# Attention, gated experts and a cosine MLP on one core: the code for the smallest slot count stands right behind its test

## The chip, the core and the metric

The kernel runs on one core of a Trainium2 chip. The metric is the device time of one execution in microseconds; lower is better. The engines are TensorE (PE in the rows, its weight loads PEld), VectorE (DVE), ScalarE (ACT), GpSimd (POOL) and SyncE (SP), which issues most transfers. A name with a q behind it (PEldq, SPq) is the engine's sequencer, the part that reads the instructions in order and deals with waits, register loads, tests and jumps.

## The reference

```
attn = softmax(q k^T / 8 + bias(position))           # 2 batches, 8 heads, 576 positions, 64 wide
x    = (attn v), heads side by side                   # 1152 tokens x 512
logits = x w_gate + log(1 + exp(x w_noise)) * noise   # 8 experts
the two largest logits of a token choose its experts; softmax over the two gives their weights
x    = sum of both: weight * relu(x w1[e]) w2[e]      # 512 -> 1024 -> 512
h    = x w_in;  out = (h cos(h)) w_out                # 512 -> 2048 -> 512
```

How many tokens an expert gets depends on the data.

## The kernel before

The first part is the attention for all 1152 tokens, in tiles of 128 tokens. While it runs, each tile's gate is computed, the two experts of a token are chosen, and a slot in the list of each of them is counted out; GpSimd then scatters the token's row to those slots in a DRAM buffer (`xg`, line 840). Each expert has room for C = 320 slots.

The second part is `experts(bctx, W, ahead)`. It runs the eight experts over W slots each, expert by expert and in each over eight blocks of 128 hidden units: twelve matmuls (each operand is split into a high and a low part) into the tile H, a relu into `hhl`, twelve matmuls into the tiles Y. The weights of each block come by SyncE (`wraw`, line 1025) and are split by ScalarE (lines 1032 and 1040) and VectorE (1036, 1042). Beside this it already loads (line 1051) and converts weights of the last part. The slots of expert 1 and later are loaded from `xg` (line 1094); expert 0's input and its first three weight blocks lie on the chip when the attention part ends. The cosine MLP follows within the same function, with three token groups, and the last four stores to the output are issued by SyncE (line 1279).

The order of instructions on each engine is fixed while the program is built, by a small planner (`Plan`) that costs every step. It knows nothing of the tests.

The matmuls of the experts take as many columns as slots are computed. So the body is built three times, for 304, 312 and 320 slots (`WIDTHS` and C), and a fourth time for 320 slots with an extra part in front, which takes what an expert gets beyond 320. Which one runs is decided on the chip: `total_i` holds the largest count of any expert (written on VectorE at line 853), every engine loads it into a register (line 1351) and tests it (lines 1352, 1353 and 1411). In each engine's stream the blocks stand one behind the other as they are written: extra part and 320, then 320, then 312, then 304, then the end of the program, with semaphores and a barrier of all engines (under the line of the surrounding context, 1499). At the end of each body a jump leads to that common end. In this input the 304-slot body runs.

Of the kernel before, what the change touches and what calls it, by code (L numbers as in the profile page):

```python
# [8 lines left out]
F32 = mybir.dt.float32  # L9
# [4 lines left out]
AF = mybir.ActivationFunctionType  # L14
OP = mybir.AluOpType
AX = mybir.AxisListType
PSUM = bass.MemoryType.PSUM

B, H, S, D = 2, 8, 576, 64
DM = H * D  # L20
NT = B * S
HID = 32
E = 8
F = 1024
FB = F // 128
# [4 lines left out]
NTILE = NT // 128  # L30
C = 320
WIDTHS = (C - 16, C - 8)
# [133 lines left out]
def attention_moe_cosine_mlp_kernel(  # L166
# [5 lines left out]
    nc = tc.nc  # L172
# [11 lines left out]
    yd = dram.tile([ROWS, DM], F32, name="yd")  # L184
    xd = dram.tile([NT, DM], F32, name="xd")
# [16 lines left out]
    ident = const.tile([128, 128], F32, name="ident")  # L202
    carry = const.tile([128, NTILE + 1, E], F32, name="carry")
    oh = const.tile([128, NTILE, 2, E], BF16, name="oh")
# [6 lines left out]
    total = const.tile([128, E + 1], F32, name="total")  # L211
    total_i = const.tile([128, 2, E + 1], I32, name="total_i")
# [13 lines left out]
    with ExitStack() as actx:  # L226
        pool = actx.enter_context(tc.tile_pool(name="attn", bufs=1))
# [5 lines left out]
                     t=[128, S], m=[128, 1], e0=[128, 640], e1=[128, S], et=[128, 4, 128], etl=[128, 128],  # L233
                     ot=[128, 4, 128], rs=[128, H], x=[128, DM], lgs=[128, 128], rt=None,
                     bias=[128, H, S])
        bufs = dict(S=2, etp=2, aux=2, qraw=2, kraw=2, feat=5, bst=2, t=3, m=4, e0=2, e1=2, et=4, etl=2, ot=2, rs=3,
                    x=3, lgs=1, rt=2, qt=3, bias=2, raw=RAWS)
# [1111 lines left out]


    most = nc.values_load(total_i[0:1, 0, E:E + 1], min_val=0, max_val=2 * NT)
    with tc.If(most > WIDTHS[1]) as more:
        with tc.If(most > C) as over:
            with tc.tile_pool(name="ovf", bufs=1) as pool, tc.tile_pool(name="ps_o", bufs=2, space=PSUM) as ps_o:
                within = pool.tile([128, NTILE, E], F32, name="within")
                nc.vector.tensor_tensor(within, carry[:, 1:NTILE + 1, :],
                                        carry[:, 0:1, :].to_broadcast([128, NTILE, E]), op=OP.subtract)
                nc.vector.tensor_scalar(within, within, float(C), None, op0=OP.is_le)
                nc.vector.tensor_reduce(total[:, 0:E], within.rearrange("p t e -> p e t"), axis=AX.X, op=OP.add)
                nc.vector.tensor_copy(total_i[:, 1, 0:E], total[:, 0:E])  # L1360
                acc = pool.tile([128, NTILE, 2, DM], F32, name="oacc")
                nc.vector.memset(acc, 0.0)
                for e in range(E):
                    count = nc.values_load(total_i[0:1, 0, e:e + 1], min_val=0, max_val=NT)
                    with tc.If(count > C):
                        w = pool.tile([128, FB, 2, 512], F32, name="ow")
                        for f in range(FB):
                            nc.sync.dma_start(w[:, f], mwp[e * FB + f].rearrange("p (a d) -> p a d", a=2))
                        t0 = nc.values_load(total_i[0:1, 1, e:e + 1], min_val=0, max_val=NTILE - 1)
                        with tc.For_i(t0, NTILE) as t:  # L1370
                            x = pool.tile([128, 4, 128], F32, name="ox")
                            src = xd[bass.ds(t * 128, 128), :]
                            if e == 0:
                                nc.sync.dma_start(x, src.rearrange("p (c s) -> p c s", c=4))
                            else:
                                src = src.rearrange("p (i c b) -> p c i b", i=4, c=4)
                                for c in range(4):
                                    nc.sync.dma_start(x[:, c].rearrange("p (i b) -> p i b", i=4), src[:, c])
                            hotf = pool.tile([128, 2, E], F32, name="ohot")
                            nc.vector.tensor_copy(hotf, oh[:, bass.ds(t, 1), :, :].rearrange("p o j e -> p (o j) e"))  # L1380
                            ps = ps_o.tile([128, 512], F32, name="otr")
                            for c in range(4):
                                nc.tensor.transpose(ps[:, c * 128:(c + 1) * 128], x[:, c, :], ident)
                            xT = pool.tile([128, 4, 128], F32, name="oxT")
                            nc.vector.tensor_copy(xT.rearrange("p c s -> p (c s)"), ps)
                            py = ps_o.tile([128, 512], F32, name="opy")
                            for f in range(FB):
                                ph = ps_o.tile([128, 512], F32, name="oph")
                                for c in range(4):
                                    nc.tensor.matmul(ph[:, 0:128], w[:, f, 0, c * 128:(c + 1) * 128], xT[:, c, :],  # L1390
                                                     start=(c == 0), stop=(c == 3))
                                hT = pool.tile([128, 128], F32, name="ohT", bufs=2)
                                nc.scalar.activation(hT, ph[:, 0:128], AF.Relu)
                                nc.tensor.matmul(py, hT, w[:, f, 1, :], start=(f == 0), stop=(f == FB - 1))
                            a = acc[:, bass.ds(t, 1), :, :].rearrange("p o j (i c b) -> p (o j) c i b", i=4, c=4)
                            yv = py.rearrange("p (c i b) -> p c i b", c=4, i=4)
                            for j in range(2):
                                for c in range(4):
                                    nc.vector.scalar_tensor_tensor(a[:, j, c], yv[:, c], hotf[:, j, e:e + 1], a[:, j, c],
                                                                   op0=OP.mult, op1=OP.add)  # L1400
                for j in range(2):
                    r = j * NT
                    nc.sync.dma_start(yd[r:r + NT, :].rearrange("(t p) d -> p t d", p=128), acc[:, :, j, :])

            with ExitStack() as bctx:
                experts(bctx, C, False)
        with over.Else():
            with ExitStack() as bctx:
                experts(bctx, C)
    with more.Else():  # L1410
        with tc.If(most > WIDTHS[0]) as some:
            with ExitStack() as bctx:
                experts(bctx, WIDTHS[1])
        with some.Else():
            with ExitStack() as bctx:
                experts(bctx, WIDTHS[0])


# [84 lines left out]
```

## Time and profile before

| | us |
|---|---|
| median of 3 runs | 681.82 (681.18 to 684.2) |
| profiled execution, its own time | 689.02 |
| span of the profiled execution | 687.2 |
| TensorE busy | 632.1 (92%) |
| VectorE busy | 510.0 (74%) |
| ScalarE busy | 395.6 (58%) |
| GpSimd busy | 107.1 (16%) |

The span runs from the first to the last instruction of the profiled execution. Busy times do not count register loads, tests, jumps and semaphores; such instructions are on record by line, though, with their start and duration. An "issue" wait is time in which an engine waited for nothing that the profile shows as work. The granted clock of TensorE (PEclk) is a share of 2.4 GHz; the mean over the span is 0.982, and it has two levels, 1 and 0.5. "q8 instruction" and "q14 instruction" are the DMA queues that bring instructions to the engines; a packet of the first has 16 KB, one of the second 8 KB.

### The profile page before, as it was taken

To read this page: it belongs to the slowest core of one execution; us is meant where nothing else is said; L and a number is where in the kernel's file an instruction comes from. 1 tells how busy PE (TensorE), PEld (TensorE's weight loads), DVE (VectorE), ACT (ScalarE), POOL (GpSimd) and SP (SyncE) were. 2 spreads that over 40 slices of the span, in tenths; PEclk is the share of its full clock that TensorE was granted. 3 is DMA by queue.
4 is the path that set the end of the run, shared out by engine and by line. 5 is a ranking of instruction groups with operands and counts; after the bars stand their busy time and mean duration, and the time that the engine had idled before them with its cause. 6 is when DMAs were issued, how large, how long until landed. Compare 5 with 4: busy or idle time off the path is not lost.

```text
span 687.2 us, 12766 instructions
## 1 busy us (share of the span) xinstructions
PE 632.1 (92%) x4678; PEld 552.3 (80%) x4678; DVE 510.0 (74%) x1271; ACT 395.6 (58%) x791; POOL 107.1 (16%) x179
## 2 busy tenths in 40 slices
PE   5778998898899849999998998999999999999996
PEld 1346676675578649999998998999999999999996
DVE  6796897898878637989969888766998545554443
ACT  5666687777668525666645646544665444444333
POOL 4140124313222210002100011021400040001000
PEclk9998999999999959999999999999999999999999
DMA  5858788676658329698897897974730040001001
GB/s 174 207 162 255 247 281 270 214 217 199 204 165 267 106 73 279 189 302 269 238 301 211 250 281 207 250 201 157 240 100 25 0 138 1 1 7 40 1 1 46
DMA packets 58177, 116.45 MB, mean 169 GB/s; under 512 B 7024, under 2 KB 26864, under 8 KB 56048
## 3 DMA queue, kind: packets, MB, share of 16 engines
q1 hardware_dynamic: 54544, 104.41, 51.1%
q0 software_dynamic: 3552, 11.04, 4.8%
q8 instruction: 41, 0.67, 0.4%
q14 instruction: 40, 0.33, 0.2%
HBM read 78.12 MB, written 32.58 MB: 161 GB/s over the span
## 4 chain that ended last, share of the span: by engine, by line
PE 51%; DMA 6%; DVE 5%; issue 2%; ACT 1%; SPq 0%; DVEq 0%; POOL 0%; ACTq 0%
PE H L1002 25%; PE Y L1002 25%; DMA wraw<-in_mwp_dram 3%; DMA io<-xg 2%; DVE qt L1042 1%; DVE whl L1042 1%; DVE io L1153 1%; DMA xg<-x,token 1%; PE H L1191 1%; DMA bias<-xg 1%; DVE s L1072 1%; DVE s L1103 0%; ACT qt L1040 0%; DVE hhl L1133 0%; DVE qraw L1108 0%
## 5 line engine op out<-in xcount | busy, mean ns | idle before, releaser
L1002 PE MATMUL Y<-hhl,qt 128*128 128x304 f32 x468 | 73.3, 302 | 4.3 <-DVE hhl L1133 4.1
L1002 PE MATMUL Y<-w,hhl 128*128 128x512 f32 (+1 forms) x330 | 74.8, 372 | 0.0
L1002 PEld LDWEIGHTS Y<-hhl,qt 128*128 128x128 f32 x468 | 66.8, 188 | 5.6 <-DVE hhl L1133 5.5
L1002 PEld LDWEIGHTS Y<-w,hhl 128*128 128x128 f32 x330 | 56.7, 188 | 8.7
L503 ACT ACTIVATE e<-t,m 128x576 f32<-128x576 f32 x72 | 55.5, 771 | 11.8 <-DVE m L494 10.6
L489 PE MATMUL S<-kt,qt 128*128 128x288 f32 x320 | 59.0, 313 | 2.9 <-DVE m L494 2.9
L494 DVE CUSTOM_DVE_ANT_0 t<-S,bias 128x576 f32<-128x576 f32 x72 | 53.4, 750 | 9.4 <-DMA bias<-e 2.7
L1002 PE MATMUL H<-qraw,qt 128*128 128x304 f32 (+1 forms) x300 | 50.9, 321 | 8.3 <-issue 8.3
L1002 PEld LDWEIGHTS H<-qraw,qt 128*128 128x128 f32 x300 | 47.9, 199 | 9.1 <-issue 8.6
L489 PEld LDWEIGHTS S<-kt,qt 128*128 128x128 f32 x320 | 45.1, 190 | 8.5 <-DVE m L494 4.1
L1131 ACT ACTIVATE hhl<-H 128x304 fp32r<-128x304 f32 x64 | 26.7, 417 | 40.3 <-PE H L1002 38.4
L1002 PE MATMUL H<-qraw,w 128*128 128x384 f32 x264 | 49.3, 336 | 0.0
L1242 ACT ACTIVATE u<-H 128x384 f32<-128x384 f32 (+1 forms) x52 | 23.8, 466 | 42.2 <-PE H L1002 40.3
L1002 PEld LDWEIGHTS H<-qraw,w 128*128 128x128 f32 x264 | 46.6, 188 | 1.7
L510 PE MATMUL etp<-ident,e 128*128 128x128 f32 x288 | 44.6, 278 | 3.3 <-ACT e L503 2.6
L538 PE MATMUL aux<-et,vt 128*64 128x128 f32 (+1 forms) x640 | 42.5, 277 | 5.5 <-DMA vt<-in_vd_dram 3.2
L1042 DVE TENSOR_TENSOR qt<-wraw,qt 128x1024 fp32r<-128x1024 f32 x35 | 42.7, 1224 | 6.2 <-ACT qt L1040 5.6
L1002 PE MATMUL Y<-hhl,whl 128*128 128x304 f32 x300 | 45.6, 300 | 0.0
L1248 ACT ACTIVATE u<-u 128x384 f32<-128x384 f32 (+1 forms) x52 | 25.7, 498 | 34.1 <-DVE u L1246 33.8
L538 PEld LDWEIGHTS aux<-et,vt 128*64 128x64 f32 x640 | 33.2, 143 | 13.7 <-DMA vt<-in_vd_dram 3.5
L1254 DVE TENSOR_TENSOR hhl<-u,hhl 128x384 fp32r<-128x384 f32 (+1 forms) x52 | 27.2, 526 | 22.7 <-ACT hhl L1252 22.0
L1040 ACT ACTIVATE qt<-wraw 128x1024 fp32r<-128x1024 f32 x36 | 37.7, 1053 | 10.5 <-DMA wraw<-in_mwp_dram 6.1
(206 smaller groups left out, 1372.6 us busy)
## 6 DMA issues: line engine op xcount, KB each, us to landing
wraw<-in_mwp_dram SPq DMA_DIRECT2D x64, 512.0 KB
r<-in_mw2p_dram SPq DMA_DIRECT2D x16, 1024.0 KB
dist<-bst SPq DMA_DIRECT2D x24, 295.5 KB
bias<-dist SPq DMA_DIRECT2D x24, 288.0 KB
xg<-zero SPq DMA_DIRECT2D x20, 256.0 KB
yd<-zero SPq DMA_DIRECT2D x20, 256.0 KB
yd<-io SPq DMA_DIRECT2D x32, 160.0 KB
io<-xg SPq DMA_DIRECT2D x28, 160.0 KB
```

Source lines behind the costliest of these rows:

```text
L489: nc.tensor.matmul(s[:, hf, 0:HF], tl("qt", (it, bb))[:, u, h, :], kt[:, bb, h, hf * HF:hf * HF + HF], start=(i == 0), stop=(i == len(term ...
L494: nc.vector.tensor_tensor_reduce(out=tl("t", n).rearrange("p (a j) -> p a j", a=2), in0=tl("S", n)[:, :, 0:HF], in1=tl("bias", it)[:, h, : ...
L503: P.op({"ACT": 0.76}, lambda e: nc.scalar.activation(tl(*ek)[:, 0:S], tl("t", n), AF.Exp, bias=tl("m", n), scale=-1.0, accum_out=tl("rs", ...
L510: nc.tensor.transpose(tl("etp", n)[:, j * 128:(j + 1) * 128], tl(*ek)[:, j * 128:(j + 1) * 128], ident)
L538: nc.tensor.matmul(tl(*ax2)[h0, q0], lw, rx, start=(s == 0), stop=(s == 4))
L1002: nc.tensor.matmul(out_, lw(a), rx(b_), start=(first and i == 0), stop=(last and i == n - 1))
L1040: P.op({"ACT": 0.947}, lambda e: nc.scalar.activation(wt(i)[:, 0], tl(*rk), AF.Copy), pr, r=[rk], w=[wname(i) + (0,)])
L1042: P.op({"DVE": 1.135, "POOL": 2.4}, lambda e: (nc.gpsimd if e == "POOL" else nc.vector).tensor_tensor(wt(i)[:, 1], tl(*rk), wt(i)[:, 0].bi ...
L1131: P.op({"ACT": 0.053 + 0.00083 * W}, lambda en: nc.scalar.activation(tl(*hk)[:, 0, 0:W], tl(*pk)[:, 0:W], AF.Relu), g + 0.3, r=ks, w=[hk + ...
L1242: P.op({"ACT": 0.06 + 0.00083 * m}, lambda e: nc.scalar.activation(u(), h(), AF.Copy, scale=1.0 / (2.0 * math.pi), bias=0.25), z, r=ks, w= ...
L1248: P.op({"ACT": 0.187 + 0.00083 * m}, lambda e: nc.scalar.activation(u(), u(), AF.Sin, scale=2.0 * math.pi), z + 0.04, r=[un[1]], w=[un[2]])
L1254: P.op({"DVE": 0.069 + 0.00104 * m}, lambda e: nc.vector.tensor_tensor(part(1), u(), part(0).bitcast(F32), op=OP.subtract), z + 0.07, r=[u ...
```

## The change

The tests are turned around and nested the other way. The first asks whether the largest count is at most 304, and the 304-slot body stands right behind it; then 312, then 320, and what goes beyond 320 comes last. The code of the four bodies is the same, the extra part is only indented differently (its lines are left out here).

```diff
     most = nc.values_load(total_i[0:1, 0, E:E + 1], min_val=0, max_val=2 * NT)
-    with tc.If(most > WIDTHS[1]) as more:
-        with tc.If(most > C) as over:
-            with tc.tile_pool(name="ovf", bufs=1) as pool, tc.tile_pool(name="ps_o", bufs=2, space=PSUM) as ps_o:
...
-            with ExitStack() as bctx:
-                experts(bctx, C, False)
-        with over.Else():
-            with ExitStack() as bctx:
-                experts(bctx, C)
-    with more.Else():
-        with tc.If(most > WIDTHS[0]) as some:
+
+    with tc.If(most <= WIDTHS[0]) as few:
+        with ExitStack() as bctx:
+            experts(bctx, WIDTHS[0])
+    with few.Else():
+        with tc.If(most <= WIDTHS[1]) as some:
             with ExitStack() as bctx:
                 experts(bctx, WIDTHS[1])
         with some.Else():
-            with ExitStack() as bctx:
-                experts(bctx, WIDTHS[0])
+            with tc.If(most <= C) as full:
+                with ExitStack() as bctx:
+                    experts(bctx, C)
+            with full.Else():
+                with tc.tile_pool(name="ovf", bufs=1) as pool, tc.tile_pool(name="ps_o", bufs=2, space=PSUM) as ps_o:
...
+                with ExitStack() as bctx:
+                    experts(bctx, C, False)
```

In TensorE's stream, the place where the count is loaded and tested, with what stands before and behind the jumps (H and Y are the tiles in PSUM, `qraw` holds the input of expert 0, `qt` the weights of the first three blocks). Before; behind the first dots come the end of the 320-slot body, the second test and the start of the 312-slot body, behind the second dots the end of the 312-slot body and the start of the 304-slot body:

```order
L639 MATMUL etp<-t,x 128x64 x8
L657 MATMUL S<-ident 128x128 x4
L1351 TENSOR_LOAD total_i
L1352 COMPARE_AND_BRANCH
L1353 COMPARE_AND_BRANCH
L1364 TENSOR_LOAD total_i
...
L1353 UNCONDITIONAL_BRANCH
L1411 COMPARE_AND_BRANCH
L1002 MATMUL H<-qraw,qt 128x312 x30
...
L1411 UNCONDITIONAL_BRANCH
L1002 MATMUL H<-qraw,qt 128x304 x30
```

In the changed kernel the same place of TensorE's stream reads:

```order
L639 MATMUL etp<-t,x 128x64 x8
L657 MATMUL S<-ident 128x128 x4
L1351 TENSOR_LOAD total_i
L1353 COMPARE_AND_BRANCH
L1002 MATMUL H<-qraw,qt 128x304 x30
L1002 MATMUL Y<-hhl,qt 128x304 x12
L1002 MATMUL H<-qraw,qt 128x304 x6
L1002 MATMUL Y<-hhl,qt 128x304 x12
```

Before, the way from the first test (L1352) to the 304-slot matmuls leads over two jumps; now these matmuls stand behind the one test (L1353).

In SyncE's stream, the end of the 304-slot body. Before, these are the last rows, and the common end of the program follows:

```order
L1051 DMA r_20459<-in_mw2p_dram 128x2048
L1051 DMA r_20561<-in_mw2p_dram 128x2048
L1279 DMA out_dram<-s 16x8x512 x2
L1279 DMA out_dram<-s 16x8x256 x2
L1411 UNCONDITIONAL_BRANCH
```

In the changed kernel the 312-slot body follows, then the other two:

```order
L1051 DMA r_6523<-in_mw2p_dram 128x2048
L1279 DMA out_dram<-s 16x8x512 x2
L1279 DMA out_dram<-s 16x8x256 x2
L1353 UNCONDITIONAL_BRANCH
L1357 COMPARE_AND_BRANCH
L1051 DMA r_7988<-in_mw2p_dram 128x2048
L1025 DMA wraw<-in_mwp_dram 128x1024 x2
```

The jump at the end of the body (L1411 before, L1353 now) went to the next instructions of the stream and now goes past three bodies.

## Rows read from the trace of the kernel before

**Rows 1.** The page: the span.
```profile
span 687.2 us, 12766 instructions
```

**Rows 2.** Chain of waits, 236 to 262 us: start, duration, what.
```profile
244.00 1.88 PE S L657 x8
245.88 8.29 issue
254.18 7.18 PE H L1002 x30
```

**Rows 3.** Table of waits, 243 to 262 us: who, for what, total, times, longest.
```profile
ACT whl L1032 <- issue: 10.2, 1, 10.2
...
PE H L1002 <- issue: 8.3, 1, 8.3
```

**Rows 4.** Line 1351: ns min/median/max, first and last start in us.
```profile
L1351 PEldq TENSOR_LOAD <-total_i x1: 487/487/487, 244.8 to 244.8; - x1
```

**Rows 5.** Line 1352, the first test.
```profile
L1352 ACTq COMPARE_BRANCH  x1: 50/50/50, 245.4 to 245.4; - x1
L1352 PEldq COMPARE_BRANCH  x1: 3458/3458/3458, 245.4 to 245.4; - x1
L1352 SPq COMPARE_BRANCH  x1: 50/50/50, 245.7 to 245.7; - x1
```

**Rows 6.** Line 1411, the second test.
```profile
L1411 ACTq COMPARE_BRANCH  x1: 45/45/45, 248.3 to 248.3; - x1
L1411 PEldq COMPARE_BRANCH  x1: 4948/4948/4948, 249.0 to 249.0; - x1
L1411 SPq COMPARE_BRANCH  x1: 45/45/45, 249.3 to 249.3; - x1
```

**Rows 7.** First instructions behind it: lines 1032, 1499 and 1002, 244 to 260 us.
```profile
L1032 ACTq EVENT_SEMAPHORE  x3: 38/38/38, 254.4 to 254.6; - x3
...
L1499 SPq EVENT_SEMAPHORE  x3: 17/17/17, 255.0 to 259.8; - x3
...
L1002 PE MATMUL H<-qraw,qt x11: 455/455/592, 254.2 to 256.8; 128*128 128x304 f32 x11
```

**Rows 8.** DMA queues, 242:254, then 262:670, then 670:688: packets, MB, share.
```profile
q14 instruction: 11, 0.09, 5.4%
q8 instruction: 3, 0.05, 2.7%
...
q8 instruction: 20, 0.33, 0.3%
...
q1 hardware_dynamic: 576, 0.79, 14.7%
```

**Rows 9.** Stretches: length, busy PE, PEld, DVE, ACT, POOL; PEclk, DMA share, GB/s.
```profile
59.00:60.00 1.00, 0.11 (x2) 0.11 (x4) 0.00 (x0) 0.00 (x0) 0.00 (x0) 0.50 0.96 245
65.00:66.00 1.00, 1.00 (x9) 0.83 (x5) 0.79 (x1) 0.86 (x4) 0.00 (x0) 0.62 0.10 37
243.00:244.00 1.00, 1.00 (x8) 1.00 (x8) 0.63 (x2) 0.34 (x1) 0.00 (x0) 0.63 0.00 0
260.00:261.00 1.00, 1.00 (x8) 1.00 (x7) 0.00 (x0) 0.42 (x1) 0.00 (x0) 0.84 0.41 135
```

**Rows 10.** The end: lines 1352 and 1499, and SyncE's waits.
```profile
L1352 ACTq EVENT_SEMAPHORE  x1: 17/17/17, 682.0 to 682.0; - x1
L1352 SPq EVENT_SEMAPHORE  x1: 17/17/17, 683.9 to 683.9; - x1
...
L1499 SPq EVENT_SEMAPHORE  x2: 28/28/28, 686.2 to 686.3; - x2
...
SPq L1499 <- DMA out_dram<-s: 1.7, 1, 1.7
```

**Rows 11.** Stretches, columns as in rows 9: the scatter over, the 1 MB load.
```profile
251.00:252.00 1.00, 0.00 (x0) 0.00 (x0) 0.00 (x0) 0.00 (x0) 0.00 (x0) 0.50 0.00 0
256.00:260.00 4.00, 4.00 (x18) 4.00 (x17) 2.74 (x4) 2.64 (x5) 0.00 (x0) 0.50 0.79 268
```

More of the change, by code (lines that the diff above doesn't have):

```diff
@@ L1351, in attention_moe_cosine_mlp_kernel @@
     most = nc.values_load(total_i[0:1, 0, E:E + 1], min_val=0, max_val=2 * NT)
-    with tc.If(most > WIDTHS[1]) as more:
-        with tc.If(most > C) as over:
-            with tc.tile_pool(name="ovf", bufs=1) as pool, tc.tile_pool(name="ps_o", bufs=2, space=PSUM) as ps_o:
[L1355 to L1403, printed above, removed]
-            with ExitStack() as bctx:
-                experts(bctx, C, False)
-        with over.Else():
-            with ExitStack() as bctx:
-                experts(bctx, C)
@@ L1414, in attention_moe_cosine_mlp_kernel @@
         with some.Else():
-            with ExitStack() as bctx:
-                experts(bctx, WIDTHS[0])
+            with tc.If(most <= C) as full:
[3 more added lines that the diff above has]
+                with tc.tile_pool(name="ovf", bufs=1) as pool, tc.tile_pool(name="ps_o", bufs=2, space=PSUM) as ps_o:
+                    within = pool.tile([128, NTILE, E], F32, name="within")
+                    nc.vector.tensor_tensor(within, carry[:, 1:NTILE + 1, :],
+                                            carry[:, 0:1, :].to_broadcast([128, NTILE, E]), op=OP.subtract)
+                    nc.vector.tensor_scalar(within, within, float(C), None, op0=OP.is_le)
+                    nc.vector.tensor_reduce(total[:, 0:E], within.rearrange("p t e -> p e t"), axis=AX.X, op=OP.add)
+                    nc.vector.tensor_copy(total_i[:, 1, 0:E], total[:, 0:E])
+                    acc = pool.tile([128, NTILE, 2, DM], F32, name="oacc")
+                    nc.vector.memset(acc, 0.0)
+                    for e in range(E):
+                        count = nc.values_load(total_i[0:1, 0, e:e + 1], min_val=0, max_val=NT)
+                        with tc.If(count > C):
+                            w = pool.tile([128, FB, 2, 512], F32, name="ow")
+                            for f in range(FB):
+                                nc.sync.dma_start(w[:, f], mwp[e * FB + f].rearrange("p (a d) -> p a d", a=2))
+                            t0 = nc.values_load(total_i[0:1, 1, e:e + 1], min_val=0, max_val=NTILE - 1)
+                            with tc.For_i(t0, NTILE) as t:
+                                x = pool.tile([128, 4, 128], F32, name="ox")
+                                src = xd[bass.ds(t * 128, 128), :]
+                                if e == 0:
+                                    nc.sync.dma_start(x, src.rearrange("p (c s) -> p c s", c=4))
+                                else:
+                                    src = src.rearrange("p (i c b) -> p c i b", i=4, c=4)
+                                    for c in range(4):
+                                        nc.sync.dma_start(x[:, c].rearrange("p (i b) -> p i b", i=4), src[:, c])
+                                hotf = pool.tile([128, 2, E], F32, name="ohot")
+                                nc.vector.tensor_copy(hotf, oh[:, bass.ds(t, 1), :, :].rearrange("p o j e -> p (o j) e"))
+                                ps = ps_o.tile([128, 512], F32, name="otr")
+                                for c in range(4):
+                                    nc.tensor.transpose(ps[:, c * 128:(c + 1) * 128], x[:, c, :], ident)
+                                xT = pool.tile([128, 4, 128], F32, name="oxT")
+                                nc.vector.tensor_copy(xT.rearrange("p c s -> p (c s)"), ps)
+                                py = ps_o.tile([128, 512], F32, name="opy")
+                                for f in range(FB):
+                                    ph = ps_o.tile([128, 512], F32, name="oph")
+                                    for c in range(4):
+                                        nc.tensor.matmul(ph[:, 0:128], w[:, f, 0, c * 128:(c + 1) * 128], xT[:, c, :],
+                                                         start=(c == 0), stop=(c == 3))
+                                    hT = pool.tile([128, 128], F32, name="ohT", bufs=2)
+                                    nc.scalar.activation(hT, ph[:, 0:128], AF.Relu)
+                                    nc.tensor.matmul(py, hT, w[:, f, 1, :], start=(f == 0), stop=(f == FB - 1))
+                                a = acc[:, bass.ds(t, 1), :, :].rearrange("p o j (i c b) -> p (o j) c i b", i=4, c=4)
+                                yv = py.rearrange("p (c i b) -> p c i b", c=4, i=4)
+                                for j in range(2):
+                                    for c in range(4):
+                                        nc.vector.scalar_tensor_tensor(a[:, j, c], yv[:, c], hotf[:, j, e:e + 1], a[:, j, c],
+                                                                       op0=OP.mult, op1=OP.add)
+                    for j in range(2):
+                        r = j * NT
+                        nc.sync.dma_start(yd[r:r + NT, :].rearrange("(t p) d -> p t d", p=128), acc[:, :, j, :])
+                with ExitStack() as bctx:
+                    experts(bctx, C, False)
```

## The prediction

> **What bounds the kernel now.** I read the chain of waits first. Around the change it goes from TensorE's last matmul of the attention part (L657, over at 245.88 us) through 8.29 us of "issue" to the first expert matmul at 254.18 [rows 2]. From there to the end the chain is TensorE work with short gaps, so an expert part that starts earlier ends earlier. The table of waits says the same by engine: TensorE idle 8.3 us, ScalarE 10.2 us, both for "issue", that is, for nothing that another engine or a transfer owes them [rows 3]; VectorE in its turn waits for ScalarE there.
>
> The rows of the branch lines say what the "issue" is. The count is loaded at 244.8 in 0.49 us on TensorE's sequencer [rows 4]. The first test follows at 245.4 and is on record with 3458 ns on TensorE; the second starts at 249.0 with 4948 ns, so it is over at 253.95 [rows 5, 6]. On ScalarE and SyncE a test itself takes 45 to 50 ns, but the next instruction comes much later: on ScalarE the tests start at 245.4 and 248.3 and the next instruction at 254.4; on SyncE at 245.7, 249.3 and 255.0 [rows 5 to 7]. So a taken jump costs 2.85 (ScalarE), 3.46 (TensorE) or 3.55 us (SyncE) the first time, and 4.95 (TensorE), 5.65 (SyncE) or 6.05 us (ScalarE) the second. In that stretch the two instruction queues of the DMA carry 14 packets in 12 us, and in the last 18 us of the run, where only near code is reached, none; only data moves [rows 8]. My reading: the jump itself is cheap, and what costs is bringing in code that lies far away.
>
> **The change, part by part.** *Head.* On every engine two tests, both jumping far, become one test that falls into the 304-slot code, which now stands right behind it. Load and test stay: on TensorE 245.4 for the test. Its last attention matmul ends at 245.88, so if falling through costs no more than the 45 to 50 ns of the test on the other engines, the first expert matmul starts at about 245.9 instead of 254.18: 8.3 us earlier. It needs nothing later: input and weights of the first three blocks are written in the attention part. The feeders move by more: ScalarE's first instruction from 254.4 to about 245.45 (9.0), SyncE's from 255.0 to 245.8 (9.2); VectorE's first work waits for ScalarE and moves with it. GpSimd's two scatters stand ahead of its test and stay.
>
> No row shows a test that is not taken, so its price lies between 0.05 us (the record of a test) and 3.46 us (a whole first jump on TensorE). I take the low end: what follows is the next instruction in the stream, and where the stream runs straight on, from 262 to 670, one instruction queue alone brings 20 packets [rows 8] while the table of waits of that stretch has no "issue" wait of TensorE.
>
> The clock adds something. TensorE's granted clock falls from 1 to 0.5 (from 2.4 to 1.2 GHz) at 243.3 (the mean 0.63 of that microsecond) and is back at 260.3 (mean 0.84), 6.1 us after the expert matmuls began; at the other such place it works again from 59.9 on and has full clock at 65.8, 5.9 us later [rows 9]. If the clock returns about 6 us after work starts again, and that start is the first matmul of the experts, all of it merely shifts, and full speed comes at 252.0. But now TensorE works on nearly without a break from 242.0; counted from there the clock is back at 247.9, which saves half of 4.1 us, 2.05. So 0 to 2.05. I take 0.5: ScalarE and VectorE move by only 9.0, and later TensorE stalls are waits for VectorE, so what goes beyond 9.0 is largely lost there. Head: 8.3 + 0.5 = **8.8 us gained**.
>
> *Tail.* The 304-slot code was the last in each engine's stream, and its end lay next to the common end of the program. Now three other bodies lie between, so each of the five engines makes one far jump at the end. Price: the same rows, 2.85 to 6.05 us. Who waits? TensorE, VectorE and ScalarE are done before SyncE: ScalarE's last semaphore before the end stands at 682.0, SyncE's at 683.9 [rows 10], so with equal jumps SyncE's ends last. SyncE issues the last stores, and now waits 1.7 us for them to land; from 686.3, when it has gone through its semaphores, 0.9 us of barrier lead to 687.2 [rows 1, 10]. A jump that starts at 683.9 runs beside the landing of the stores and covers that wait, so it is not added whole. I take 4.0 us: SyncE's first jump was 3.55, and here the stores keep the DMA busy. Then 687.9; some 14 semaphores of the common end, at the pace of the last ones about 0.05 each, 0.6; the barrier 0.9: 689.4 instead of 687.2, **2.2 us lost**. With 2.85 it is 1.1 lost, with 6.05 4.3.
>
> *Everything else.* The instructions of the 304-slot body are the same in number and order, so matmuls, transfers and waits within it shift as a block. The 1 MB load that opens SyncE's part now starts beside the last scatter; 268 GB/s over 256 to 260 us makes it some 4 us of DMA, the scatter's packets end before 251 [rows 11]; the loads that need the scatter come for the second expert only, so I cost this at nothing. Without that cover it could hold SyncE's queue for at most those 4 us.
>
> **Sum.** The profiled execution took 689.02 us with a span of 687.2 [rows 1]: 689.02 - 8.8 + 2.2 = 682.4, that is 6.6 us less. It stands 7.2 us above the median of the runs, 681.82; a code fetch should cost about the same in either, so I carry the difference over: 681.82 - 6.6 = **675.2 us**.
>
> [...]
>
> **The rivals.**
> 1. *A test costs its fetch even when not taken.* The head then gains 8.3 less one first jump of 2.85 to 3.46, about 5.1, the tail still loses 2.2: 678.9 us (678.6 to 679.2). For it: TensorE's record shows the long time on the test itself, not behind it. Against: on the other engines the test is 45 to 50 ns and the pause comes behind.
> 2. *The clock comes back early and its gain is kept.* Head 10.35, tail 1.1 to 2.2: 672.6 to 673.7 us. For it: no break in TensorE's work at the seam any more. Against: the later waits for VectorE.
> 3. *Jumps are cheap, and the long records are an effect of taking the profile.* Then an unprofiled run saves one test of 50 ns [rows 5]: 681.8 us, and the change does not do what it seems to. [...] Against: the engines really do nothing in 246 to 254, and the instruction queues move packets there.
> 4. *The start is held by the scatter, and the tail pays: slower.* SyncE's 1 MB load, started at 246, collides with the last scatter and pushes its landing from about 250 by up to 4 us to 254. If the first expert work waits on it, the head gains nothing (254.2), and an end jump at the upper price costs 4.3: 686.1 us. It decides once the first expert matmul comes later than about 252, that is, once the gain ahead falls under the 2.2 of the tail. For it: the scatter does end just ahead of the present start. Against: the wait table names no transfer ahead of the first matmul.
>
> That the count is above 304 in this input, so that other code is run, is out: the first expert matmuls have 304 columns [rows 7].
>
> **How the numbers follow.** Forecast 0.74, rival 1 0.09, rival 2 0.08, rival 3 0.05, rival 4 0.04. A measurement of this kernel can tell about 0.5% from no change, 3.4 us. Forecast and rival 2 are faster: 0.82. Rivals 1 and 3 end within it: 0.14. Slower: 0.04. The low end of the range is rival 2 at its best, 8.3 + 2.05 gained and 1.1 lost, 672.5. The worst of the forecast's own bounds is 8.3 - 4.3 = 4.0 gained, 677.8; reaching to the near edge of rival 1 gives 678.6. Left out are most of rival 1, rivals 3 and 4, and a little of the scatter of runs: under 2 in 10.
>
> **What would show it.** In the changed profile: one test per engine, of some 50 ns; TensorE's first expert matmul at about 246, ScalarE's first conversion at 245.7; few instruction packets in 242 to 254; full clock by 252 at the latest. At the end SyncE's last stores some 8.8 us earlier, at about 675, then a pause of 3 to 6 us on SyncE with instruction packets in it, and no wait for the stores. Wrong would be: a pause of several us behind the test (rival 1), a first matmul that waits for a transfer (rival 4), an end where TensorE's or ScalarE's jump ends after SyncE's, or stalls in 260 to 430 us that grow by several us and eat the head's gain.

## The result and the profile after

| | median, us | runs |
|---|---|---|
| kernel before, same chip | 684.38 (681.18 to 690.47) | 12 |
| changed kernel | 675.73 (671.15 to 680.18) | 12 |

The ratio is 0.9892, 95% interval 0.9859 to 0.9924: the changed kernel is about 1.1% faster, 7.4 us by the ratio. The forecast was 675.2 us and 6.6 us less. Two more comparisons on other occasions gave 0.9902 (0.987 to 0.9934) and 0.9874 (0.9845 to 0.9903). Runs over 1.5% above a kernel's fastest count as slow and are left out of the ratios, which concerns only two of the six runs of one_jump_hint further below (680.07, its profiled run, and 678.45 us).

The page of the changed kernel, its span (against [rows 1]):

```profile
span 669.3 us, 12766 instructions
```

The difference of these two spans, 17.9 us, is not the effect of the change. The runs of either kernel scatter by some 9 us, and these two executions lie near opposite ends. Both have to be cut into parts before they are compared.

In the timeline of the changed kernel at the seam (start, duration, engine, line, operation; in brackets the idle time before it and who ended it) the count is ready when line 853 ends, and the experts begin with the first matmul of line 1002. In the kernel before, where that matmul starts at 254.18 [rows 2], line 853 reads:

```profile
244.65 0.16 DVE L853 CAST total_i<-total 128x9 int32<-128x9 f32 x1
```

In the changed kernel:

```profile
238.48 2.05 PE L657 MATMUL S<-ident 128*128 128x128 f32 x8
...
239.06 0.16 DVE L853 CAST total_i<-total 128x9 int32<-128x9 f32 x1
...
240.22 1.10 PE L1002 MATMUL H<-qraw,qt 128*128 128x304 f32 x3
240.29 0.63 ACT L1032 ACTIVATE whl<-wraw 128x512 fp32r<-128x512 f32 x1 [1.14 <-DVE token L857]
```

The matmul begins 1.16 us behind the start of the cast, where the kernel before had 9.5. There is no pause on TensorE any more; ScalarE idles 1.1 us where it idled 10.2 [rows 3]. The line of the test shows why. In its rows (nanoseconds min, median and max, then the first and last start in us) there are now two records for each engine, the test at the head and the jump at the end of the body:

```profile
L1353 ACTq COMPARE_BRANCH  x2: 38/41/44, 239.8 to 662.9; - x2
L1353 PEldq COMPARE_BRANCH  x2: 95/1864/3633, 239.9 to 660.3; - x2
L1353 SPq COMPARE_BRANCH  x2: 41/47/53, 240.1 to 664.8; - x2
...
L1353 SPq EVENT_SEMAPHORE  x1: 17/17/17, 664.7 to 664.7; - x1
```

On TensorE the test that falls through took 95 ns. The 3633 ns are the far jump at the end, on record like the first test of before, 3458 ns [rows 5]. The count is loaded as before [rows 4]:

```profile
L1351 PEldq TENSOR_LOAD <-total_i x1: 487/487/487, 239.3 to 239.3; - x1
```

The table of waits, TensorE alone, from 236 to 300 us, has one line, and no "issue":

```profile
PE Y L1002 <- DVE hhl L1133: 1.1, 1, 1.1
```

Stretches around the seam (columns as in [rows 9]):

```profile
234.00:235.00 1.00, 0.55 (x3) 0.31 (x3) 0.80 (x7) 0.07 (x1) 0.00 (x0) 1.00 0.71 250
235.00:236.00 1.00, 0.72 (x7) 0.60 (x8) 0.00 (x0) 0.62 (x2) 0.00 (x0) 0.53 0.05 20
...
241.00:242.00 1.00, 1.00 (x6) 1.00 (x5) 0.79 (x2) 0.98 (x2) 0.78 (x3) 0.55 1.22 131
242.00:243.00 1.00, 1.00 (x9) 1.00 (x8) 1.00 (x1) 1.00 (x1) 0.66 (x1) 1.00 0.48 115
```

The clock falls to half at about 235, while TensorE has small gaps, and is back at 241.9, 1.7 us behind the first expert matmul instead of 6.1 [rows 9].

The end. SyncE's wait for its stores, 1.7 us before [rows 10], has become 0.3 in the table of waits of its queue; the line of the common end (now 1500) shows when each engine is through its jump:

```profile
SPq L1500 <- DMA out_dram<-s: 0.3, 1, 0.3
```

```profile
L1500 SPq EVENT_SEMAPHORE  x14: 17/28/28, 667.4 to 669.3; - x14
...
L1500 PEldq DRAIN  x2: 8/40/73, 664.0 to 668.8; - x2
L1500 ACTq DRAIN  x2: 8/44/80, 666.3 to 668.8; - x2
L1500 DVEq DRAIN  x2: 10/34/57, 666.6 to 668.8; - x2
```

SyncE's jump starts at 664.8 and its next instruction comes at 667.4, 2.6 us later; it is the last engine through. From its semaphore to the end of the span it is 4.6 us (664.7 to 669.3), where it was 3.3 (683.9 to 687.2): 1.3 us lost. The DMA queues in this last stretch, 664 to 670, carry instruction packets, where [rows 8] has none:

```profile
q1 hardware_dynamic: 514, 0.66, 34.2%
q14 instruction: 6, 0.05, 2.6%
q8 instruction: 1, 0.02, 1.4%
```

Cut in this way, with two more profiles of the kernel before and two of the changed one (lead: from the start of the cast at line 853 to the first expert matmul; body: from there to the first store of line 1279; end: from there to the end of the span; stalls: TensorE's idle time in the body):

| profile | attention | lead | body | stalls in it | end |
|---|---|---|---|---|---|
| before | 244.6 | 9.53 | 427.0 | 5.4 | 6.0 |
| before_2 | 237.9 | 9.85 | 423.4 | 3.4 | 6.0 |
| before_3 | 239.2 | 9.86 | 426.8 | 5.1 | 6.0 |
| changed | 239.1 | 1.16 | 421.8 | 2.9 | 7.3 |
| after_2 | 237.6 | 1.16 | 422.2 | 3.0 | 6.9 |
| after_3 | 237.8 | 1.16 | 430.6 | 8.0 | 7.4 |

Lead and end are the same within 0.5 us in every profile of a kernel; attention and body scatter by 7 and 9 us, the first although the change does not touch it. So of the 17.9 us of the first pair 8.4 are the lead and -1.3 the end; 5.6 come from the attention part and 5.2 from the body, which the other profiles don't bear out. By the means, the lead gives 9.75 - 1.16 = 8.6 us and the end takes 7.2 - 6.0 = 1.2: **7.4 us**, which is what the ratio says.

### The profile page after: what moved, and what is told of

Read it like the earlier page. It is cut to its first block, busy times and chain, and to the rows that moved or that the text cites. A ratio compares the mean times of both kernels' runs of the same rounds, so it can differ in the third digit from the quotient of the medians.

```text
span 669.3 us, 12766 instructions
## 1 busy us (share of the span) xinstructions
PE 631.3 (94%) x4678; PEld 550.8 (82%) x4678; DVE 511.0 (76%) x1271; ACT 395.4 (59%) x791; POOL 107.2 (16%) x179
## 4 chain that ended last, share of the span: by engine, by line
PE 44%; DVE 8%; DMA 7%; issue 1%; ACT 1%; SPq 0%; DVEq 0%
PE Y L1002 22%; PE H L1002 22%; DMA wraw<-in_mwp_dram 3%; DMA io<-xg 3%; DVE qt L1042 1%; DVE whl L1042 1%; DVE s L1103 1%; DMA r<-in_mw2p_dram 1%; DVE io L1153 1%; DVE hhl L1133 1%; DVE s L1072 1%; DMA yd<-io 1%; ACT whl L1040 1%; PE H L1191 1%; DVE qraw L1108 1%
## 5 line engine op out<-in xcount | busy, mean ns | idle before, releaser
L1002 PE MATMUL H<-qraw,qt 128*128 128x304 f32 (+1 forms) x300 | 48.9, 312 | 0.0
L1002 PEld LDWEIGHTS H<-qraw,qt 128*128 128x128 f32 x300 | 45.9, 191 | 0.5
L510 PEld LDWEIGHTS etp<-ident,e 128*128 128x128 f32 x288 | 33.5, 143 | 13.1 <-ACT e L503 5.5
L1244 DVE TENSOR_SCALAR s<-u 128x384 f32<-128x384 f32 (+1 forms) x52 | 17.8, 345 | 34.0 <-ACT u L1242 34.0
```

The lines of the kernel that those rows point to most:

```text
L510: nc.tensor.transpose(tl("etp", n)[:, j * 128:(j + 1) * 128], tl(*ek)[:, j * 128:(j + 1) * 128], ident)
L1002: nc.tensor.matmul(out_, lw(a), rx(b_), start=(first and i == 0), stop=(last and i == n - 1))
L1244: P.op({"DVE": 0.069 + 0.00052 * m}, lambda e: nc.vector.tensor_scalar(k(), u(), MAGIC, MAGIC, op0=OP.add, op1=OP.subtract), z + 0.01, r=[ ...
```

## The experiments

Each ratio is to the kernel before on the same chip and occasion (medians there 686.98 us for the first four kernels, 681.54 for one_jump_hint and after_2, 681.84 for one_jump_hint_2 and after_3).

**The price of a jump: one, three or none.** Three kernels hold the same four bodies and reach the 304-slot one in different ways. The first has it last, behind one jump:

```diff
-    with tc.If(most <= WIDTHS[0]) as few:
+    with tc.If(most > WIDTHS[0]) as other:
...
+    with other.Else():
+        with ExitStack() as bctx:
+            experts(bctx, WIDTHS[0])
```

> Layout of before (304-slot body last, near the common end), but one test that jumps straight to it instead of two. Theory (each far jump at the head costs 3 to 5 us, a near end costs nothing): from the load of the count to the first expert matmul 4.3 to 4.9 us (before 9.4, changed kernel 0.9), the end as before (3.3 us from SyncE's last semaphore of the body to the end of the span), in all 4 to 6 us under before. Rival (the gain comes from something else than the jumps, such as where the code happens to lie): time as before, within 2 us. Rival (only the second jump is dear): 0.9 plus 4.95, about 5.9 us from load to matmul, and 3.5 us under before.

Measured: 684.37 us, ratio 0.9949 (0.9912 to 0.9986). By the ratio that is 3.5 us under the kernel before (1.0 to 6.0), a little less than the 4 to 6 expected; so the time alone would also suit the second rival, and the lead decides. Lead 4.61 us, which is 4.4 from the load, as the theory had it and not 5.9; end 6.0. Its one taken test is 3545 ns long on TensorE, and 50 ns on ScalarE with the pause behind it (ScalarE's next work starts at 246.1):

```profile
L1352 ACTq COMPARE_BRANCH  x1: 50/50/50, 243.1 to 243.1; - x1
L1352 PEldq COMPARE_BRANCH  x1: 3545/3545/3545, 243.2 to 243.2; - x1
```

So one far jump costs 4.61 - 1.16 = 3.5 us, and taking away the second of the two was worth 9.75 - 4.61 = 5.1 (9.75 is the mean lead of the kernel before). Distance alone does not set this price: the jump of 3.5 us goes past three bodies, the second jump of the kernel before, 4.95 us on TensorE [rows 6], past one. The second kernel asks for more than 320 first, then more than 312, then more than 304, and jumps each time:

```diff
-    with tc.If(most <= WIDTHS[0]) as few:
+    with tc.If(most > C) as over:
...
+    with over.Else():
+        with tc.If(most > WIDTHS[1]) as more:
...
+        with more.Else():
+            with tc.If(most > WIDTHS[0]) as some:
...
+            with some.Else():
+                with ExitStack() as bctx:
+                    experts(bctx, WIDTHS[0])
```

> The layout of before with three tests that all jump far, instead of two, in the order above 320, above 312, above 304. Theory: a third far jump adds 3 to 5 us, so 12.5 to 14.5 us from the load of the count to the first expert matmul and 3 to 5 us over before. Rival (the time at the head is one latency that the jumps share): 9.4 us and the time of before.

Measured: 694.56 us, ratio 1.0103 (1.0066 to 1.014), slower than the kernel before by 7.1 us; lead 15.50 us (15.3 from the load), end 6.0. Both are over what was expected, 3 to 5 and 12.5 to 14.5, but the rival of one shared latency is out. TensorE's three tests, each of a line of its own:

```profile
L1352 PEldq COMPARE_BRANCH  x1: 3758/3758/3758, 244.0 to 244.0; - x1
...
L1407 PEldq COMPARE_BRANCH  x1: 5604/5604/5604, 247.8 to 247.8; - x1
...
L1411 PEldq COMPARE_BRANCH  x1: 4952/4952/4952, 253.4 to 253.4; - x1
```

Every far jump adds to the lead: 3.5, 5.1 and 5.8 us by the differences of the leads. The later ones are dearer than the first; that the third is dearer than the second is not shown, for in this profile TensorE has 5.60 us on the second and 4.95 on the third. The instruction packets of the head grow with the jumps. They are counted here in the 20 us behind the start of the cast at line 853 ([rows 8] ends before the last of them):

| kernel, stretch in us | far jumps | packets of q14 | of q8 |
|---|---|---|---|
| changed, 239.06 to 259.06 | 0 | 0 | 1 |
| one_jump, 242.41 to 262.41 | 1 | 8 | 3 |
| before, 244.65 to 264.65 | 2 | 14 | 5 |
| three_jumps, 243.16 to 263.16 | 3 | 21 | 6 |

The third kernel has the same number of tests as the second, but all three fall through, into the 304-slot body:

```diff
-    with tc.If(most <= WIDTHS[0]) as few:
-        with ExitStack() as bctx:
-            experts(bctx, WIDTHS[0])
-    with few.Else():
+    with tc.If(most <= C) as full:
+        with tc.If(most <= WIDTHS[1]) as some:
+            with tc.If(most <= WIDTHS[0]) as few:
+                with ExitStack() as bctx:
+                    experts(bctx, WIDTHS[0])
```

> Three tests that all fall through (at most 320, at most 312, at most 304), then the 304-slot body, and the far jump at its end. Theory (a test that falls through costs about its own 50 to 100 ns): 1.1 to 1.2 us from the load to the first expert matmul, time within 1 us of the changed kernel, 6 to 9 us under before. Rival (the prediction's first: a test costs its fetch even when it falls through, and only the first one was covered): two more tests cost 6 to 7 us, time as before.

Measured: 679.43 us, ratio 0.9887 (0.9841 to 0.9934), that of the changed kernel. Lead 1.41, end 7.2. The tests on TensorE (of the third line the median is the mean of the test and the jump at the end):

```profile
L1352 PEldq COMPARE_BRANCH  x1: 98/98/98, 245.0 to 245.0; - x1
...
L1353 PEldq COMPARE_BRANCH  x1: 64/64/64, 245.1 to 245.1; - x1
...
L1354 PEldq COMPARE_BRANCH  x2: 64/1696/3328, 245.2 to 664.6; - x2
```

Two more tests cost 1.41 - 1.16 = 0.25 us, some 0.12 each. Rival 1, a test that costs its fetch even when it is not taken, is out: by its bounds, 2.85 to 3.46 us a test, two more of them would have put some 6 us into this lead.

**No test at all.** The fourth kernel has only the 304-slot body, without load, test or jumps; it leaves out the code for larger counts.

```diff
-    most = nc.values_load(total_i[0:1, 0, E:E + 1], min_val=0, max_val=2 * NT)
-
-    with tc.If(most <= WIDTHS[0]) as few:
-        with ExitStack() as bctx:
-            experts(bctx, WIDTHS[0])
-    with few.Else():
...
+    with ExitStack() as bctx:
+        experts(bctx, WIDTHS[0])
```

> No load of the count, no test and no jump: only the 304-slot body is in the program (the code for larger counts is left out). Theory: the first expert matmul follows the attention part directly, the end is that of before (3.3 us) and not 4.6: 1 to 2 us under the changed kernel, 8 to 11 us under before. Rival (the far jump at the end is fully covered by the landing of the stores): the changed kernel's time within 0.5 us.

Measured: 674.74 us, ratio 0.983 (0.9775 to 0.9886). Lead 0.23, end 6.3:

```profile
240.79 1.14 PE L657 MATMUL S<-ident 128*128 128x128 f32 x8
242.26 1.97 PE L1002 MATMUL H<-qraw,qt 128*128 128x304 f32 x12 [0.34 <-DVE total_i L853]
```

Against the changed kernel that is 0.9 us at the lead (the load of 0.49 and the test among it) and 0.6 to 1.1 at the end, together under 2 us: what the choice at run time still costs. By the ratio the kernel is 11.7 us under the one before, a little more than the 8 to 11 expected and than its two ends explain, but the interval reaches down to 7.8. The rival, an end jump that is fully covered, is out by the end, 6.3 against 6.9 to 7.4; the times alone could not decide it. The jumps were what mattered, not the choice as such.

**The jump kept, with a hint ahead of it.** one_jump again, with an instruction at the very start of TensorE's, ScalarE's, VectorE's and SyncE's streams that names the branch as likely taken:

```diff
+    tc.mark_branch_hint_location("small", "LikelyTaken", engines=[mybir.EngineType.PE, mybir.EngineType.Activation, mybir.EngineType.DVE, mybir.EngineType.SP])
     most = nc.values_load(total_i[0:1, 0, E:E + 1], min_val=0, max_val=2 * NT)
-    with tc.If(most > WIDTHS[0]) as other:
+    with tc.If(most > WIDTHS[0], label="small") as few:
...
-    with other.Else():
+    with few.Else():
```

> The kernel with one far jump at the head and the 304-slot body last, and on four engines (not GpSimd) a prefetch hint for that jump; the build places it at the very start of each engine's program, the only place it would go. Theory (the jump costs the fetch of far code, and a hint fetches it ahead): 1.1 to 1.6 us from the count to the first expert matmul instead of 4.6, with the near end of 6.0 us behind the first of the last stores: 1 to 2 us under the changed kernel. Rival (a hint that far ahead is lost again, since hundreds of instructions pass in between): 4.6 us, the time of the kernel with one jump.

Measured: 672.83 us, ratio 0.9844 (0.9801 to 0.9886). Lead 1.47 instead of 4.61, with the body still standing last and the end still 6.0. That a hint given some 240 us ahead would be lost did not come true. TensorE's record of the same taken jump, from a second profile of this kernel:

```profile
L1353 PEldq COMPARE_BRANCH  x1: 392/392/392, 237.6 to 237.6; - x1
```

392 ns instead of 3545 for a jump to the same distance: neither the distance nor the branch itself is what costs. This fits the reading that the time is a wait for code that isn't there yet. In the 20 us behind the cast the instruction queues q14 and q8 carry 5 and 2 packets with the hint, where one_jump has 8 and 3, and none of them falls into the lead. That the hint brought the missing code ahead is an inference, though: in either kernel these queues carry 14 and 16 packets from the start of the span to the test, so no fetch of its own is on record for the hint. By its two ends this kernel should be 0.5 to 1 us faster than the changed one, so both were run again, beside the changed kernel run a second and a third time:

> The changed kernel once more, for its scatter. From the count to the first expert matmul 1.0 to 1.3 us, the end 7.2 to 7.4 us behind the first of the last stores, full clock within 4 us of the first expert matmul. If the fewer TensorE stalls in the body (2.9 us in the first profile, 5.4 before) belong to the change, they are again under 4 us; if they are chance, they lie anywhere between 1 and 6.

> The kernel one_jump_hint again, with more runs, beside the changed kernel again. In the first profiles the hinted kernel starts its experts 1.5 us behind the counts (changed kernel 1.1) and ends 6.0 us behind the first of the last scatters (changed kernel 6.9 and 7.3), so its two ends together are 0.5 to 0.9 us shorter; against that stands an expert part of 432.7 us in its one profile, where the changed kernel had 421.8 and 422.2. If the long expert part is scatter: the profile shows an expert part of 421 to 427 us, and the ratio to the kernel before lies within 0.003 of the changed kernel's, rather below it. If the hint itself lengthens the expert part: again about 430 us or more with 9 us of idle time of TensorE, and a ratio at least 0.01 above the changed kernel's.

> The changed kernel again, beside the hinted one. Its ratio to the kernel before was 0.9892 and 0.9902: again 0.987 to 0.993. The profile: experts start 1.1 us behind the counts, the expert part is 421 to 425 us, the last part 6.9 to 7.3 us, and the full clock comes 1 to 3 us behind the start of the experts, where the kernel before had it 4 to 6 us behind.

| kernel | median, us | ratio, interval | lead | body | stalls | end |
|---|---|---|---|---|---|---|
| one_jump_hint | 672.83 | 0.9844 (0.9801 to 0.9886) | 1.47 | 432.7 | 9.4 | 6.0 |
| after_2 | 674.23 | 0.9902 (0.987 to 0.9934) | 1.16 | 422.2 | 3.0 | 6.9 |
| one_jump_hint_2 | 675.18 | 0.9899 (0.986 to 0.9939) | 1.46 | 430.9 | 8.6 | 6.0 |
| after_3 | 672.85 | 0.9874 (0.9845 to 0.9903) | 1.16 | 430.6 | 8.0 | 7.4 |

The first two and the last two rows were measured together. Once the hinted kernel is ahead, once the changed one, and the intervals overlap both times: the two can't be told apart, and a version that beats the changed kernel is not shown. The long body of about 431 us need not be the hint's doing either: after_3 has it without a hint, while its ratio is the lowest of the three of the changed kernel. It came again in one_jump_hint_2, against the first expectation of that run, but the ratio 0.01 above, which the second wanted, did not. The body of after_3 missed its 421 to 425 us, and its clock was full before the experts began, not 1 to 3 us into them. After_2, with 3.0 us of stalls and an end of 6.9 (7.2 to 7.4 expected), could not tell whether short stalls belong to the change; the 8.0 of after_3 say that they need not. TensorE's waits from 240 to 660 us, first in the profile of the changed kernel, then in after_3:

```profile
PE Y L1002 <- DVE hhl L1133: 2.1, 3, 1.1
PE H L1002 <- DVE whl L1042: 0.7, 1, 0.7
```

```profile
PE Y L1002 <- DVE hhl L1133: 6.7, 8, 2.1
PE H L1002 <- DVE whl L1042: 0.7, 1, 0.7
PE H L1002 <- DVE qraw L1108: 0.2, 1, 0.2
```

The same code waits three times or eight for VectorE's relu. In after_3 the longest of these waits, 2.1 us up to 349.1, is followed by a stretch at half clock, from 350.3 to 353.7 us; the first two profiles of the changed kernel have none in the body behind 242 us. What decides this from one execution to the next was not tried.

**The kernel before, two more profiles**, for the scatter of its parts:

> The kernel before once more, for its scatter. From the count to the first expert matmul 9 to 10 us, the end 6.0 us, the body some 427 us if its stalls belong to the late start, otherwise anywhere from 422 to 428; the count ready at 238 to 246 us, since the part ahead of it is untouched by the change.

> A third profile of the kernel before, with the same expectations as for the second.

They took 678.84 and 683.72 us, with spans of 677.1 and 681.9; their parts stand in the table of the first section. Lead and end repeat (9.85 and 9.86; 6.0 and 6.0), body and attention do not.

## Why the prediction was right, step by step

*The head, 8.3.* Right: 8.4 in the first pair, 8.6 by the means. The rows of the branch lines could be read as they stood: a pause at each taken far jump, 2.85 to 3.55 us the first time and 4.95 to 6.05 the second, on every engine that feeds the start. The price of a test that falls through was taken at its low end, 0.05 us, and is 0.03 to 0.1 in its record, some 0.12 in the lead. The reason given for it left something out: from 262 to 670 us the second instruction queue brings another 12 packets beside the 20 of [rows 8], still without an "issue" wait. On TensorE a test that jumps far has 3545 ns (one_jump), one that falls through 64 to 98 (changed kernel and three_falls), with 34 to 60 on the other engines.

*Rival 3*, long records that are only an effect of taking the profile, forecast no change of the time. By the medians and ratios of all runs the change saves 6.7, 7.4 and 8.6 us in its three comparisons, and three_jumps is slower than the kernel before by about 7, so the jumps do cost measured time. As span and clock are on record for every run, no run is known to have gone without any recording, and whether the recording itself lengthens a jump is not shown.

*The clock, 0.5.* Not seen in the time. At half clock a 304-column matmul starts every 253 ns in the trace of before (22 steps from 254.57 to 260.14 us), 1.2 columns a ns, which is how it shows the prediction's 1.2 GHz; at full clock it is every 138 ns (28 steps from 260.92 to 264.78), 2.2 columns a ns. The half clock reaches 6.1, 4.5 and 3.6 us into the experts in the three profiles of before, and 1.7, 1.3 and 0 in those of the changed kernel. By the means that is some 3.7 us less of half clock, by itself worth an estimated 1.7 at the two paces. It speaks for rival 2's premise, that the clock comes back early, but weakly: three_falls, without a pause at the seam too, has the half clock 3.9 us into the experts, and the two hinted profiles 2.6 and 3.8. Nor do the 6 us from the first matmul to full clock, from which the term was worked out, repeat in the other two profiles of before (4.5 and 3.6). Rival 2's conclusion, that the gain is kept, is not to be seen: the bodies are 425.7 us before and 424.9 after in the mean, and scatter by 9, and the shortest of all, 420.6 in three_falls, follows one of the later returns of the clock. The lead and the end alone make up the 7.4 us of the ratio. The prediction let most of this gain be lost in later waits for VectorE; the waits that vary are indeed those, but that they ate the clock's gain is an inference, not shown.

*The tail, -2.2.* Right in sign and mechanism, too large: 1.2. The step that failed in size is the price of SyncE's jump, put at 4.0 us because "here the stores keep the DMA busy"; it took 2.6 in the profile of the changed kernel (664.8 to 667.4), less than the lower bound of 2.85 too. SyncE's first jump at the head of the kernel before took 3.55 [rows 5, 6], so beside the stores a jump was not dearer, and their landing was nearly covered by it, as forecast (0.3 us of wait left of 1.7). That SyncE would be the last engine through was right, by 0.8 us: VectorE's jump took 4.0 us (662.6 to 666.6) but began 2.2 earlier.

*Everything else, 0.* Right. The 1 MB load, issued at 240.4, does run beside GpSimd's last two scatters (issued at 240.4 and 241.7, the first landing 6.6 us later), but the first expert matmul had begun at 240.2 and waits for neither. So rival 4, a start held by the scatter, is out.

*The sum.* 8.3 + 0.5 - 2.2 = 6.6 against a measured 7.4, with -0.5 for the clock that didn't show, +1.0 for the tail and +0.3 for the head, which is 7.4. The errors of the clock and of the tail partly cancel; the ratio's interval, about 2.2 us to either side, couldn't have told any of them, only the parts could. That 675.2 us lies so near the measured 675.73 is in part luck: it starts from 681.82, the median of three runs of the kernel before, 2.6 us under that of all twelve.

## What to carry to other kernels

Here an "issue" wait around a branch, with packets on the instruction queues, came and went with the far jumps: where a profile shows one, put the body that runs most often right behind its test, so that the test falls through, and count the jumps on the way to it, since each cost 3.5 to 5.8 us here. The far jump that this put at the end of the body cost only 1.2 us beside the landing of the last stores. Larger counts were not run: by the order of the tests, counts of 313 to 320 now meet two far jumps where they met one. And when the parts that a change touches repeat to half a microsecond while the rest scatters by nine, compare the parts, and let the ratio only confirm their sum.

## What was not expected

- A hint at the start of the program, some 240 us ahead of the jump, brought TensorE's record from 3545 to 392 ns and the lead from 4.61 to 1.5 us, at the same place in the code.
- Behind a first far jump the next ones are dearer: 3.5, 5.1 and 5.8 us by the leads of the four kernels with none to three of them, though a jump past one body cost more than one past three.
- A far jump on SyncE beside its own stores took 2.6 us, less than SyncE's first jump at the head of the kernel before, 3.55.
